# Attention value products widened from 64 to 128 rows, transposes grouped by unit, first score tile at 128 columns

## The chip, the cores and the metric

The kernel runs on one core of a Trainium2 chip. The metric is the device time of one execution in microseconds (us). Three runs of the kernel before took 1123.78, 1124.84 and 1125.99 us; the median, 1124.84 us, is the time that a changed kernel is compared with.

## The reference, cut to what matters

Attention over 4 batches of 8 heads with 576 positions and head size 64, then two feed-forward layers on the 2304 tokens:

```python
scores = q @ k.T / sqrt(64)                       # per batch and head
cum    = cumsum(max(s, 0))                        # per batch and head
bias   = min(-(cum[:, None] - cum[None, :]), 0)
attn   = softmax(where(causal, -1e9, scores + bias))
x      = (attn @ v) as [2304, 512]                # heads side by side
x      = (silu(x @ w_gate) * (x @ w_val)) @ w_out # d_ff 1536
out    = silu(x @ w_in) @ w_out2                  # d_ff 2048
```

All data are float32. The kernel gets the precision of float32 out of the matrix engine by splitting an operand into a high part and the remainder (names ending in `h` and `l`, type fp32r) and adding the products.

## The kernel before, in words

**Attention.** A head's 576 positions are cut into five tiles, `TILES`: the first has 64 positions, the other four 128. A head is worked on in two units: half A is query tiles 0, 1, 2 (320 queries), half B is query tiles 3 and 4 (256 queries). There are 64 units. Each goes through three steps, in three successive slots:

1. `a_scores` (L208 on), once for each query tile: products of the queries and keys (L223), the bias and the running minimum on DVE (L231), the exponential on ACT (L241), the normalisation of `e` on POOL (L116 by way of `copy`). For query tile 0 the stationary operand has 64 columns, one for each query, and 64 key columns stream past it.
2. `a_transpose` (L257 on): PE transposes the 64 or 128 row blocks of `e` (L271) into a PSUM bank, and the bank is emptied into SBUF, ACT writing the high part `ph` (L280) and DVE the remainder `pl` (L281). `GROUPS` says which key tiles share a bank: half A has two groups, half B three. Each group is a piece of work of its own. In batch 0 (`WHOLE_P`) the weights stay float32 in one part, and L114 or L112 empties the bank.
3. `a_pv` (L288 on): for each key tile j the product of its values and the transposed weights, high part and then remainder, all added up in one bank (L299). Key tile 0 has 64 positions, so its two products run over 64 rows, with `vsa` as stationary operand (`vra` in batch 0); the others run over 128 rows with `vsb`. Then ACT and DVE take the sum out (L313, L314).

`a_split` (L178 on) makes the split operands of the next head, `vsa` and `vsb` among them. `ps_a` is the pool of four PSUM banks that scores, transposes and value products share; `pt` has four buffers each for `ph` and `pl`; `e` has six buffers.

**Order.** `slot_pieces(u)` lists the pieces of slot u: the scores of unit u, the split and load of coming heads, the value products of unit u-2, the transposes of unit u-1. The first 18 slots (batch 0 and the start of batch 1) run with no other matrix work. After that the first feed-forward layer runs in 36 chunks of weights, nine for each batch (`gate`, L413 to L415 with `pgv`; `down`, the same lines with `po`), and the pieces of two slots are dealt out between the four or eight steps of a chunk. So the attention of batches 1, 2 and 3 runs between the products of batches 0, 1 and 2. The last nine chunks and the second layer (`up2`, `down2`) have no attention in them.

The program is built with a planner that simulates the engines and may move an instruction that is ready ahead of one that waits for data or a buffer; on each engine the instructions then run in the planned order.

Of the kernel before, what the change touches and what calls it, by code (L numbers as in the profile page):

```python
# [8 lines left out]
F32 = mybir.dt.float32  # L9
F32R = mybir.dt.float32r  # L10
U32 = mybir.dt.uint32
AF = mybir.ActivationFunctionType
ALU = mybir.AluOpType

B, H, S, D = 4, 8, 576, 64
NT, DM = B * S, H * D
F1, F2 = 1536, 2048
P = 128
# [12 lines left out]
TILES = [(0, 64), (64, 128), (192, 128), (320, 128), (448, 128)]  # L31
HALF = {"A": ([0, 1, 2], 0, 320), "B": ([3, 4], 320, 256)}

GROUPS = {"A": [(0,), (1, 2)], "B": [(0,), (1, 2), (3, 4)]}
# [6 lines left out]
WHOLE_P = [(0, h) for h in range(8)]  # L41
# [4 lines left out]
VHI = "agaa"  # L46
# [21 lines left out]
def kernel(  # L68
# [15 lines left out]
    def pool(name, bufs, space=None, scope=ctx, side="left"):  # L84
        kw = {"space": space} if space is not None else {}
        return scope.enter_context(tc.tile_pool(name=name, bufs=bufs, side=side, reuse_waits="tile", **kw))
# [12 lines left out]
    qks_p = pool("qks", 2, scope=attention, side="right")  # L99
    cum_p = pool("cum", 2, scope=attention, side="right")  # L100
    e_p = pool("e", 6, scope=attention, side="right")
    pt_p = pool("pt", 4, scope=attention, side="right")
    v_p = pool("v", 2, scope=attention, side="right")
    xr_p = pool("xr", 2, scope=attention, side="right")
    xq_p = pool("xq", 2, scope=attention, side="right")
# [12 lines left out]

    ident = const.tile([P, P], F32, name="ident")
    make_identity(nc, ident)  # L120
    cum = const.tile([B * H, S], F32, name="cum")
    cum_d = dram.tile([B * H, S], F32, name="cum_d")
    w32 = dram.tile([NGV + NO1, P, CW], F32, name="w32")
    x2_d = dram.tile([KD, P, NT], F32, name="x2_d")
# [19 lines left out]


    st, loads = {}, []

    def a_load(b, h, halves):
        k1, v1, q0 = SPAN[halves]
# [28 lines left out]
    def a_split(b, h, halves):  # L178
        k1, v1, q0 = SPAN[halves]
        t, c, xa, xb = st.pop((b, h, halves))  # L180
        if (b, h) in WHOLE_S:
            ks, qs = t[:D, 1], (t[:D, 0],)
        else:
            ks = qks_p.tile([P, S], F32R, tag="ks", name="ks")
            qh = qks_p.tile([P, S], F32R, tag="qh", name="qh")
            ql = qks_p.tile([P, S], F32R, tag="ql", name="ql")
            qs = (qh, ql)
            copy(KHI[b], ks[:, :k1], t[:, 1, :k1])
            copy(QHI[b], qh[:, q0:k1], t[:, 0, q0:k1])
            eng = nc.gpsimd if b in POOL_KS else nc.vector  # L190
            eng.tensor_tensor(out=ks[D:P, :k1], in0=t[D:P, 1, :k1], in1=ks[D:P, :k1].bitcast(F32), op=ALU.subtract)
            eng = nc.gpsimd if b in POOL_QL else nc.vector
            eng.tensor_tensor(out=ql[:, q0:k1], in0=t[:, 0, q0:k1], in1=qh[:, q0:k1].bitcast(F32), op=ALU.subtract)
        if (b, h) not in WHOLE_P:
            va_s = v_p.tile([64, 2, D], F32R, tag="vsa", name="vsa")
            vb_s = v_p.tile([P, 4, 2, D], F32R, tag="vsb", name="vsb")
            copy(VHI[b], va_s[:, 0, :], xa)
            copy(VHI[b], vb_s[:, :v1, 0, :], xb[:, :v1])
            nc.vector.tensor_tensor(out=va_s[:, 1, :], in0=xa, in1=va_s[:, 0, :].bitcast(F32), op=ALU.subtract)
            eng = nc.gpsimd if b in POOL_V else nc.vector  # L200
            eng.tensor_tensor(
                out=vb_s[:, :v1, 1, :], in0=xb[:, :v1], in1=vb_s[:, :v1, 0, :].bitcast(F32), op=ALU.subtract
            )
            xa, xb = va_s.rearrange("p t d -> p (t d)"), vb_s.rearrange("p j t d -> p j (t d)")
        for half in halves:
            st[b, h, half, "in"] = (ks, qs, c, xa, xb)

    def a_scores(b, h, half, i):  # L208
        ks, qs, c, _, _ = st[b, h, half, "in"]
        q0, r = TILES[i]  # L210
        wd = q0 + r
        e = e_p.tile([P, S], F32, tag="e", name="e")

        g0 = 0 if wd <= 320 else 320
        nc.gpsimd.affine_select(
            out=e[:r, g0:wd], in_=c[:r, g0:wd], pattern=[[-1, wd - g0]], compare_op=ALU.is_ge,
            fill=-8.0 * QMASK, base=q0 - g0, channel_multiplier=1,
        )
        m = None
        for c0, n in ((0, wd),) if wd <= 512 else ((0, g0), (g0, wd - g0)):  # L220
            ps = ps_a.tile([P, 512], F32, tag="a", name="psc")
            for part, q in enumerate(qs):
                nc.tensor.matmul(  # L223
                    out=ps[:r, :n], lhsT=q[:, q0 : q0 + r], rhs=ks[:, c0 : c0 + n],
                    start=(part == 0), stop=(part == len(qs) - 1),
                )
            for g, end, gate in ((c0, min(g0, c0 + n), c), (max(g0, c0), c0 + n, e)):
                if g >= end:
                    continue
                m2 = sm_p.tile([P, 1], F32, tag="m", name="m")  # L230
                nc.vector.tensor_tensor_reduce(  # L231
                    out=e[:r, g:end], in0=ps[:r, g - c0 : end - c0], in1=gate[:r, g:end], scale=-0.125,
                    scalar=3.0e38 if m is None else m[:r], op0=ALU.add, op1=ALU.min, accum_out=m2[:r],
                )
                m = m2

        if i in (0, 1, 3):
            st[b, h, "l"] = sm_p.tile([P, 2], F32, tag="l", name="l")
        l = st[b, h, "l"]
        col = 1 if i in (2, 4) else 0  # L240
        nc.scalar.activation(  # L241
            out=e[:r, :wd], in_=e[:r, :wd], func=AF.Exp, bias=m[:r], scale=-1.0, accum_out=l[:r, col : col + 1]
        )
        st[b, h, "e", i] = e
        if i in (1, 3):
            return
        done = (0,) if i == 0 else (i - 1, i)
        w = len(done)
        rl = sm_p.tile([P, 2], F32, tag="rl", name="rl")
        nc.vector.tensor_scalar(out=l[:r, :w], in0=l[:r, :w], scalar1=1.0e-9, scalar2=None, op0=ALU.add)  # L250
        nc.vector.reciprocal(out=rl[:r, :w], in_=l[:r, :w])  # L251
        for n, j in enumerate(done):
            q0, r = TILES[j]
            e = st[b, h, "e", j]
            copy("g", e[:r, : q0 + r], e[:r, : q0 + r], rl[:r, n : n + 1])

    def a_transpose(b, h, half, js):  # L257
        tiles, base, n = HALF[half]
        ps = ps_a.tile([P, 512], F32, tag="a", name="ptr")
        kw = TILES[js[0]][1]  # L260
        at, put = 0, []
        for j in js:
            k0 = TILES[j][0]
            lo = max(k0, base)
            for i in tiles:
                q0, r = TILES[i]
                if q0 < k0:
                    continue
                e = st[b, h, "e", i]
                o = at + q0 - lo  # L270
                nc.tensor.transpose(ps[:kw, o : o + r], e[:r, k0 : k0 + kw], ident[:r, :r])  # L271
            put.append((j, at, lo - base, base + n - lo))
            at += base + n - lo
        ph = pt_p.tile([P, 512], F32 if (b, h) in WHOLE_P else F32R, tag="ph", name="ph")
        parts = (ph,)
        if (b, h) in WHOLE_P:
            copy("v" if (half, js[0]) in DVE_PT else "a", ph[:kw, :at], ps[:kw, :at])
        else:
            pl = pt_p.tile([P, 512], F32R, tag="pl", name="pl")
            nc.scalar.activation(out=ph[:kw, :at], in_=ps[:kw, :at], func=AF.Copy)  # L280
            nc.vector.tensor_tensor(  # L281
                out=pl[:kw, :at], in0=ps[:kw, :at], in1=ph[:kw, :at].bitcast(F32), op=ALU.subtract
            )
            parts = (ph, pl)
        for j, o, off, width in put:
            st[b, h, "p", half, j] = ([p[:kw, o : o + width] for p in parts], off, width)

    def a_pv(b, h, half):  # L288
        tiles, base, n = HALF[half]
# [226 lines left out]
    def slot_pieces(u):  # L516
        pcs = []
        if u < len(units):
            b, h, half, sp = units[u]
            for i in HALF[half][0]:  # L520
                pcs.append(lambda b=b, h=h, half=half, i=i: a_scores(b, h, half, i))
            if half == sp[0]:
                n = spans.index((b, h, sp))
                if n + 1 < len(spans):
                    pcs.append(lambda x=spans[n + 1]: a_split(*x))
                if n + 2 < len(spans):
                    pcs.append(lambda x=spans[n + 2]: a_load(*x))
        if u >= 2 and u - 2 < len(units):
            x = units[u - 2][:3]
            pcs.append(lambda x=x: a_pv(*x))  # L530
        if 1 <= u and u - 1 < len(units):
            b, h, half, _ = units[u - 1]
            for js in GROUPS[half]:
                pcs.append(lambda b=b, h=h, half=half, js=js: a_transpose(b, h, half, js))
        return pcs

    def w_ahead(c):
# [5 lines left out]

    def body():
        setup()
        a_load(*spans[0])
        a_load(*spans[1])
        a_split(*spans[0])
# [98 lines left out]
```

## Time and profile before

| | |
|---|---|
| runs, us | 1123.78, 1124.84, 1125.99 |
| profiled execution, us | 1128.98, its span 1127.2 |
| mean granted TensorE clock | 0.991 of full |
| PE busy | 1091.4 us (97% of the span), 6760 products |
| PE weight loads (PEld) | 996.5 us |
| DVE, ACT, POOL busy | 726.0, 589.3, 562.7 us |
| packets of DMA queue q1, share of the time of 16 DMA engines | 35.9% |

The profiled execution is one execution; its time is 1.78 us more than its span, and 4.14 us above the median of the runs. A product's duration in the trace overlaps the next one's, since the matrix engine is pipelined; what a product costs there is read from the distance of its start to the next start. In a name such as `64*128 64x320`, the first pair is the stationary operand's rows and columns, the second the streamed operand's.

### The profile page before, as it was taken

How to read it: one execution, taken by the hardware profiler on the slowest of the kernel's cores; microseconds unless marked ns; L12 is line 12 of the kernel's file. 1: busy time of each engine (PE TensorE's matmuls, PEld its weight loads, DVE VectorE, ACT ScalarE, POOL GpSimd, SP SyncE). 2: the span in 40 equal slices, each digit the busy share in tenths (PEclk: the TensorE clock that was granted, in tenths of full speed). 3: DMA queues.
4: the chain of work that ended last, by engine and by line, in shares of the span. 5: the costliest groups of instructions: out<-in, count | busy, mean ns of one | idle time of the engine just before them, and what ended most of it. 6: DMA issues, size and time to landing. Idle time of an engine off the chain costs nothing. (4 is left out here: it accounts for less than half of the span.)

```text
span 1127.2 us, 19389 instructions
## 1 busy us (share of the span) xinstructions
PE 1091.4 (97%) x6760; PEld 996.5 (88%) x6760; DVE 726.0 (64%) x1625; ACT 589.3 (52%) x1294; POOL 562.7 (50%) x603
## 2 busy tenths in 40 slices
PE   6988998999999999999999999999999999999998
PEld 4556887989999999999999999989888898988887
DVE  6777999897787887777755435734463646544333
ACT  4877887765666654666644434565242323422221
POOL 5668889895575755665632533333323232232221
PEclk9988999999999999999999999999999999999999
DMA  5587666665344445352216231721120101000012
GB/s 133 139 240 237 191 219 199 209 197 154 112 110 115 112 112 155 83 141 65 76 54 203 85 102 63 242 69 43 34 74 19 57 19 56 19 1 1 1 57 112
DMA packets 53728, 121.39 MB, mean 108 GB/s; under 512 B 8256, under 2 KB 21568, under 8 KB 53632
## 3 DMA queue, kind: packets, MB, share of 16 engines
q1 hardware_dynamic: 53632, 120.17, 35.9%
q8 instruction: 53, 0.87, 0.3%
q14 instruction: 43, 0.35, 0.1%
HBM read 101.20 MB, written 18.95 MB: 107 GB/s over the span
## 5 line engine op out<-in xcount | busy, mean ns | idle before, releaser
L428 POOL TENSOR_TENSOR h<-u,h 128x288 fp32r<-128x288 f32 (+2 forms) x176 | 192.7, 1096 | 341.0 <-ACT h L112 338.7
L413 PE MATMUL pgv<-xt,wh 128*128 128x288 f32 x768 | 231.7, 302 | 3.0 <-DVE u L424 3.0
L413 PE MATMUL po<-h,wh 128*128 128x288 f32 (+2 forms) x704 | 232.7, 332 | 1.2 <-ACT h L112 1.2
L414 PE MATMUL po<-h,wh 128*128 128x288 f32 (+2 forms) x704 | 233.1, 331 | 0.0
L415 PE MATMUL po<-h,wl 128*128 128x288 f32 (+2 forms) x704 | 231.9, 330 | 0.0
L414 PE MATMUL pgv<-xt,wh 128*128 128x288 f32 x768 | 229.2, 299 | 1.3 <-DVE xt L320 1.3
L415 PE MATMUL pgv<-xt,wl 128*128 128x288 f32 x768 | 229.0, 298 | 0.0
L402 POOL TENSOR_TENSOR wl<-wraw,wh 128x1024 fp32r<-128x1024 f32 x53 | 129.9, 2453 | 83.4 <-ACT wh L112 82.7
L413 PEld LDWEIGHTS pgv<-xt,wh 128*128 128x128 f32 x768 | 146.0, 190 | 4.5 <-DVE u L424 3.9
L414 PEld LDWEIGHTS pgv<-xt,wh 128*128 128x128 f32 x768 | 146.1, 190 | 1.8 <-DVE xt L320 1.5
L415 PEld LDWEIGHTS pgv<-xt,wl 128*128 128x128 f32 x768 | 145.8, 190 | 0.3 <-issue 0.2
L424 DVE SCALAR_TENSOR_TENSOR u<-th,pu 128x464 f32<-128x464 f32 (+1 forms) x80 | 50.6, 633 | 138.7 <-ACT th L422 138.7
L413 PEld LDWEIGHTS po<-h,wh 128*128 128x128 f32 x704 | 132.0, 188 | 8.8 <-ACT h L112 2.0
L415 PEld LDWEIGHTS po<-h,wl 128*128 128x128 f32 x704 | 132.2, 188 | 6.9
L414 PEld LDWEIGHTS po<-h,wh 128*128 128x128 f32 x704 | 132.3, 188 | 6.7 <-POOL h L428 0.4
L112 ACT ACTIVATE h<-u 128x288 fp32r<-128x288 f32 (+2 forms) x176 | 89.1, 506 | 88.9 <-DVE u L424 50.4
L116 POOL TENSOR_SCALAR e<-e,rl 64x64 f32<-64x64 f32 (+4 forms) x160 | 101.9, 647 | 57.6 <-DVE rl L251 42.5
L508 DVE SCALAR_TENSOR_TENSOR acc<-po,acc 128x464 f32<-128x464 f32 (+1 forms) x140 | 88.4, 636 | 61.8 <-PE po L415 61.3
L422 ACT ACTIVATE th<-pu 128x464 f32<-128x464 f32 (+1 forms) x80 | 44.1, 551 | 151.2 <-PE pu L415 151.2
L112 ACT ACTIVATE wh<-wraw 128x1024 fp32r<-128x1024 f32 x88 | 92.1, 1055 | 54.5 <-PE po L414 35.4
L414 PE MATMUL pu<-x,wh 128*128 128x464 f32 (+1 forms) x320 | 118.9, 371 | 0.0
L241 ACT ACTIVATE e<-e,m 64x64 f32<-64x64 f32 (+4 forms) x160 | 89.1, 557 | 56.9 <-DVE m L231 55.9
(83 smaller groups left out, 2122.2 us busy)
## 6 DMA issues: line engine op xcount, KB each, us to landing
wraw<-w SPq DMA_DIRECT2D x54, 512.0 KB, 4.5
r<-in_w_dram SPq DMA_DIRECT2D x52, 512.0 KB, 4.9
qkr<-in_qk_dram SPq DMA_DIRECT2D x64, 288.0 KB, 4.6
w<-wraw SPq DMA_DIRECT2D x18, 512.0 KB, 3.9
cumb<-cum_d SPq DMA_DIRECT2D x30, 288.0 KB, 3.4
r<-in_w_dram SPq DMA_DIRECT2D x32, 256.0 KB, 3.1
x_d<-acc SPq DMA_DIRECT2D x32, 144.0 KB, 3.9
vrb<-in_vb_dram SPq DMA_DIRECT2D x32, 128.0 KB, 4.0
```

The source lines that it names most:

```text
L112: nc.scalar.activation(out=out, in_=in_, func=AF.Copy, scale=scale)
L116: nc.gpsimd.tensor_scalar(out=out, in0=in_, scalar1=scale, scalar2=1.0, op0=ALU.mult, op1=ALU.mult)
L241: nc.scalar.activation(out=e[:r, :wd], in_=e[:r, :wd], func=AF.Exp, bias=m[:r], scale=-1.0, accum_out=l[:r, col : col + 1])
L402: engines[eng].tensor_tensor(out=wl, in0=t, in1=wh.bitcast(F32), op=ALU.subtract)
L413: nc.tensor.matmul(out=ps[:, :n], lhsT=a, rhs=xh, start=(k == 0), stop=False)
L414: nc.tensor.matmul(out=ps[:, :n], lhsT=a, rhs=xl, start=False, stop=False)
L415: nc.tensor.matmul(out=ps[:, :n], lhsT=c, rhs=xh, start=False, stop=(k == last))
L422: nc.scalar.activation(out=th[:, :n], in_=pg[:, :n], func=AF.Tanh, scale=0.5)
L424: nc.vector.scalar_tensor_tensor(out=u, in0=th[:, :n], scalar=1.0, in1=pg[:, :n], op0=ALU.add, op1=ALU.mult)
L428: engines[LO[ph]].tensor_tensor(out=lo, in0=u, in1=hi.bitcast(F32), op=ALU.subtract)
L508: nc.vector.scalar_tensor_tensor(out=a, in0=ps[:, :n], scalar=0.5, in1=a, op0=ALU.mult, op1=ALU.add)
```

## The change

Four things are done.

- The value operand and the transposed weights of key tile 0 get 128 rows, of which rows 64 to 127 are zero, in batches 1 to 3. The buffers for this (three of `vsa`, one pair `ph`, `pl` for half A and one for half B) are filled with zeros once, on POOL, by `zeros()` right after `setup()`, and only their first 64 rows are written afterwards.
- `a_transpose` takes a whole unit: all transposes of its two or three groups are issued first, each group in its own bank, and then the banks are emptied.
- The score products always use 128 query columns, so query tile 0 computes 128 columns of which 64 are used.
- Buffers: `pt` has three buffers instead of four, and `cum` lies in the pool `e`.

```diff
-    pt_p = pool("pt", 4, scope=attention, side="right")
+    pt_p = pool("pt", 3, scope=attention, side="right")
+    zero_p = pool("zero", 1, scope=attention, side="right")
-    cum = const.tile([B * H, S], F32, name="cum")
+    cum = e_p.tile([B * H, S], F32, tag="e", name="cum")
+    first_v, first_p = [], []
+
+    def zeros():
+        z = e_p.tile([P, S], F32, tag="e", name="z")
+        nc.gpsimd.memset(z[D:P], 0.0)
+        for n in range(3):
+            va_s = zero_p.tile([P, 2, D], F32R, tag=f"v0_{n}", name="vsa")
+            copy("g", va_s[D:P], z[D:P, : 2 * D].rearrange("p (t d) -> p t d", t=2))
+            first_v.append(va_s)
+            if n == 2:
+                break
+            both = []
+            for part in "hl":
+                t = zero_p.tile([P, 320], F32R, tag=f"p{part}0_{n}", name=f"p{part}0")
+                copy("g", t[D:P], z[D:P, :320])
+                both.append(t)
+            first_p.append(both)
 # a_split
-            va_s = v_p.tile([64, 2, D], F32R, tag="vsa", name="vsa")
+            va_s = first_v[(b * H + h) % 3]
-            copy(VHI[b], va_s[:, 0, :], xa)
+            copy(VHI[b], va_s[:D, 0, :], xa)
 # a_scores
-                    out=ps[:r, :n], lhsT=q[:, q0 : q0 + r], rhs=ks[:, c0 : c0 + n],
+                    out=ps[:, :n], lhsT=q[:, q0 : q0 + P], rhs=ks[:, c0 : c0 + n],
 # a_transpose: the transposes of a group as before, then
-    def a_transpose(b, h, half, js):
+    def a_transpose(b, h, half):
+        done = []
+        for js in GROUPS[half]:
...
+            done.append((js, ps, kw, at, put))
+        for js, ps, kw, at, put in done:
+            whole = (b, h) in WHOLE_P
+            if js == (0,) and not whole:
+                ph, pl = first_p["AB".index(half)]
+                rows = P
+            else:
+                ph = pt_p.tile([P, 512], F32 if whole else F32R, tag="ph", name="ph")
+                pl = None if whole else pt_p.tile([P, 512], F32R, tag="pl", name="pl")
+                rows = kw
...
+                st[b, h, "p", half, j] = ([p[:rows, o : o + width] for p in parts], off, width)
 # slot_pieces
-            for js in GROUPS[half]:
-                pcs.append(lambda b=b, h=h, half=half, js=js: a_transpose(b, h, half, js))
+            pcs.append(lambda b=b, h=h, half=half: a_transpose(b, h, half))
 # body
         setup()
+        zeros()
```

## Rows read from the trace of the kernel before

**Rows 1.** Busy time of each engine in three stretches (us from the start).

```profile
0.00:80.00 80.00, 65.05 (x302) 41.75 (x303) 59.07 (x193) 55.68 (x148) 48.90 (x91) 0.95 0.62 161
80.00:255.00 175.00, 161.74 (x1106) 146.05 (x1105) 155.12 (x382) 131.99 (x304) 152.93 (x154) 0.97 0.69 212
255.00:610.00 355.00, 353.26 (x2620) 339.14 (x2618) 266.37 (x677) 208.99 (x505) 201.47 (x240) 1.00 0.40 114
```

**Rows 2.** Timeline of PE: a value product of half B, batch 3 (start, duration).

```profile
406.73 0.29 PE L414 MATMUL po<-h,wh 128*128 128x288 f32 x1
406.87 0.29 PE L415 MATMUL po<-h,wl 128*128 128x288 f32 x1
407.09 0.38 PE L299 MATMUL pv<-ph,vsa 64*128 64x256 f32 x1
407.31 0.28 PE L299 MATMUL pv<-pl,vsa 64*128 64x256 f32 x1
407.51 0.39 PE L299 MATMUL pv<-ph,vsb 128*128 128x256 f32 x1
407.74 0.28 PE L299 MATMUL pv<-pl,vsb 128*128 128x256 f32 x1
407.86 0.28 PE L299 MATMUL pv<-ph,vsb 128*128 128x256 f32 x1
```

**Rows 3.** Timeline of the weight loads, same place.

```profile
407.09 0.18 PEld L299 LDWEIGHTS pv<-ph,vsa 64*128 64x128 f32 x1 [0.17 <-PE po L414]
```

**Rows 4.** Timeline of PE: a value product of half A.

```profile
416.49 0.41 PE L299 MATMUL pv<-ph,vsa 64*128 64x320 f32 x1
416.74 0.31 PE L299 MATMUL pv<-pl,vsa 64*128 64x320 f32 x1
416.97 0.39 PE L299 MATMUL pv<-ph,vsb 128*128 128x256 f32 x1
417.20 0.28 PE L299 MATMUL pv<-pl,vsb 128*128 128x256 f32 x1
```

**Rows 5.** Instructions on the tile vsa between 255 and 640 us.

```profile
L299 PE MATMUL pv<-ph,vsa x33: 381/384/412, 263.7 to 587.6; 64*128 64x256 f32 x17, 64*128 64x320 f32 x16
```

**Rows 6.** PE and weight loads, timeline: the first score tile of a head.

```profile
412.50 0.19 PE L223 MATMUL psc<-ks,qh 128*64 128x64 f32 x1
412.55 0.19 PEld L413 LDWEIGHTS pgv<-xt,wh 128*128 128x128 f32 x1
412.80 0.30 PE L414 MATMUL pgv<-xt,wh 128*128 128x288 f32 x1
```

**Rows 7.** Timeline of PE: a run of six transposes, and two runs of three.

```profile
408.59 0.91 PE L271 MATMUL ptr<-ident,e 64*64 64x64 f32 x6
409.47 0.29 PE L414 MATMUL pgv<-xt,wh 128*128 128x288 f32 x1
428.03 0.58 PE L271 MATMUL ptr<-ident,e 64*64 64x64 f32 x3
428.59 0.30 PE L413 MATMUL po<-h,wh 128*128 128x288 f32 x1
429.12 0.49 PE L271 MATMUL ptr<-ident,e 128*128 128x128 f32 x3
429.58 0.29 PE L415 MATMUL po<-h,wl 128*128 128x288 f32 x1
```

**Rows 8.** Timelines of ACT and DVE: emptying a bank of transposes.

```profile
421.50 0.60 ACT L280 ACTIVATE ph<-ptr 128x512 fp32r<-128x512 f32 x1 [1.54 <-PE ptr L271]
422.14 0.69 DVE L281 TENSOR_TENSOR pl<-ptr,ph 128x512 fp32r<-128x512 f32 x1 [0.61 <-ACT ph L280]
```

**Rows 9.** Waits between 80 and 260 us: total, times, longest.

```profile
PE ptr L271 <- POOL e L116: 5.9, 7, 1.4
```

**Rows 10.** POOL: its idle stretch at the start, and a copy's mean (ns).

```profile
6.94 1.40 POOL L193 TENSOR_TENSOR ql<-qkr,qh 128x576 fp32r<-128x576 f32 x1 [5.63 <-DVE qh L114]
L116 POOL TENSOR_SCALAR e<-e,rl 128x320 f32<-128x320 f32 x32 | 17.2, 538 | 0.0
```

More of the change, by code (lines that the diff above doesn't have):

```diff
@@ L194, in a_split @@
         if (b, h) not in WHOLE_P:
-            va_s = v_p.tile([64, 2, D], F32R, tag="vsa", name="vsa")
+            va_s = first_v[(b * H + h) % 3]
             vb_s = v_p.tile([P, 4, 2, D], F32R, tag="vsb", name="vsb")
-            copy(VHI[b], va_s[:, 0, :], xa)
+            copy(VHI[b], va_s[:D, 0, :], xa)
             copy(VHI[b], vb_s[:, :v1, 0, :], xb[:, :v1])
-            nc.vector.tensor_tensor(out=va_s[:, 1, :], in0=xa, in1=va_s[:, 0, :].bitcast(F32), op=ALU.subtract)
+            nc.vector.tensor_tensor(out=va_s[:D, 1, :], in0=xa, in1=va_s[:D, 0, :].bitcast(F32), op=ALU.subtract)
             eng = nc.gpsimd if b in POOL_V else nc.vector
@@ L255, in a_scores @@
             copy("g", e[:r, : q0 + r], e[:r, : q0 + r], rl[:r, n : n + 1])
-    def a_transpose(b, h, half, js):
+    def a_transpose(b, h, half):
         tiles, base, n = HALF[half]
[L259 to L286, printed above, removed]
@@ new lines, in a_transpose @@
+        done = []
+        for js in GROUPS[half]:
+            ps = ps_a.tile([P, 512], F32, tag="a", name="ptr")
+            kw = TILES[js[0]][1]
+            at, put = 0, []
+            for j in js:
+                k0 = TILES[j][0]
+                lo = max(k0, base)
+                for i in tiles:
+                    q0, r = TILES[i]
+                    if q0 < k0:
+                        continue
+                    e = st[b, h, "e", i]
+                    o = at + q0 - lo
+                    nc.tensor.transpose(ps[:kw, o : o + r], e[:r, k0 : k0 + kw], ident[:r, :r])
+                put.append((j, at, lo - base, base + n - lo))
+                at += base + n - lo
+            done.append((js, ps, kw, at, put))
@@ new lines, in a_transpose @@
+        for js, ps, kw, at, put in done:
[7 more added lines that the diff above has]
+                rows = kw
+            parts = (ph,)
+            if whole:
+                copy("v" if (half, js[0]) in DVE_PT else "a", ph[:kw, :at], ps[:kw, :at])
+            else:
+                nc.scalar.activation(out=ph[:kw, :at], in_=ps[:kw, :at], func=AF.Copy)
+                nc.vector.tensor_tensor(
+                    out=pl[:kw, :at], in0=ps[:kw, :at], in1=ph[:kw, :at].bitcast(F32), op=ALU.subtract
+                )
+                parts = (ph, pl)
+            for j, o, off, width in put:
+                st[b, h, "p", half, j] = ([p[:rows, o : o + width] for p in parts], off, width)
```

## The prediction

> **What bounds the kernel now.** I read the busy times by stage first. Between 255 and 610 us PE is busy 353.26 of 355 us at full clock, DVE 266.37, ACT 208.99, POOL 201.47 [rows 1]: there PE alone sets the pace, and what shortens PE's work shortens the kernel. Between 80 and 255 us PE is still first with 161.74 of 175, but DVE (155.12) and POOL (152.93) are close behind it [rows 1]: an engine that is handed less work there may just wait longer. In the first 80 us PE is busy 65.05 of 80 [rows 1]. This is batch 0, whose value products the change leaves at 64 rows. After 610 us there is no attention, so nothing of the change acts there.
>
> Second came the timeline of PE inside the middle stage. A busy PE is not PE at its peak, so I read distances between starts. Two gate products of 288 columns start 0.14 us apart (406.73, 406.87), and two value products of 256 columns over 128 rows 0.12 apart (407.74, 407.86) [rows 2]. Around the two products of key tile 0, the distances are longer: 406.87 to 407.09, 0.22; to 407.31, 0.22; to 407.51, 0.20; to 407.74, 0.23 [rows 2]. The weight loads tell why. The load for the first `vsa` product begins only at 407.09, after its queue sat idle for 0.17 us until the product before had ended [rows 3]. Elsewhere a load runs under the product before it. So going from 128 rows to 64 empties the pipeline and then leaves a load uncovered, and going back to 128 rows does it again. Half A shows the same: 0.25, 0.23 and 0.23 us [rows 4].
>
> **The change part by part.**
>
> *Value products of key tile 0.* With 128 rows the columns streamed stay the same, so the products should start at the distances of their neighbours. Half B: 0.22 becomes 0.14, 0.22 becomes 0.12, 0.20 becomes 0.12, 0.23 becomes 0.12; together 0.87 becomes 0.50, a gain of 0.37 us for a unit [rows 2]. Half A: 256 columns take 0.12, so 320 take about 0.15, an estimate; 0.25 and 0.23 become 0.15 each, 0.23 becomes 0.12, and the entry gains 0.08 as in half B; together 0.37 [rows 2, 4]. Batches 1 to 3 have 24 heads, so 48 units; 33 of them start after 255 us [rows 5]. There the gain is whole: 33 x 0.37 = 12.2 us. The 15 earlier units could give 15 x 0.37 = 5.6 us, or nothing if DVE and POOL decide; PE is the busiest of the three, so I take two thirds, 3.7 us.
>
> *First score tile with 128 query columns.* The streamed work stays at 64 columns; the weight load doubles. Now the pair and the gate product behind it take 412.50 to 412.80, 0.30 us; less 0.14 for the gate product that leaves 0.16 for the pair [rows 6, 2]. The nearest row for a load of 128 columns in front of a short product is the run of three transposes of 128 columns: 429.12 to 429.58, less 0.14, is 0.32, or 0.11 each [rows 7, 2]. A pair would then take 0.22, that is 0.06 more for a head; 32 heads, 1.9 us. From below it costs nothing; I take 1.5, since PE is not the bound everywhere.
>
> This is where a rule speaks for a larger gain. In the trace the load of the gate weights behind the 64-column pair starts at 412.55, 0.05 us after the first of the pair, with no idle time in front of it [rows 6]: a stationary operand of 64 columns does not empty the pipeline, one of 64 rows does. The Trainium skill (TensorEngine Tiling (Array Packing), Tiling Modes, Key Properties) says that changing the tiling mode drains the engine, and counts 128x64 among the modes as it does 64x128. By that rule this edit would take away two drains for each head, and the sum would be lower, as the rival on columns below says; by the row it costs.
>
> *Transposes in one run.* A run of six takes 408.59 to 409.47, 0.88, less 0.14: 0.74. Two runs of three take 428.03 to 428.59 (0.42) and 429.12 to 429.58 (0.32), also 0.74 [rows 7, 2]. So a longer run saves nothing of PE's own time: I take 0. The 64-row transpose of query tile 0 stays, with its drain. What moves is the place: with fewer pieces in a chunk, the transposes of half B come later behind the scores, and those of its first group no longer stand a step ahead of the rest. Between 80 and 260 us PE stood 5.9 us, 7 times, before a transpose that waited for POOL's normalisation [rows 9]; this could shrink, a gain of at most 5.9. Against it, a run in half B holds three of the four banks of `ps_a` at once, and a bank is free only after ACT and DVE have emptied it, 0.60 and 0.69 us for the widest [rows 8]. Behind a PE instruction that waits for a bank everything on PE is queued. In the middle stage the planner has gate products, which use other banks, to put in front of it. Net 0.
>
> *Zeros and buffers.* One memset and seven copies on POOL; the nearest row is 0.54 us for 128x320, so 8 x 0.54 = 4.3 us. POOL sits idle for 5.63 us before its first work of the attention [rows 10], and this covers them. If they ran in front of the first score tile's masks instead, up to 4.3 us. The zeros' first readers are in batch 1. `pt` loses a buffer, but key tile 0 no longer uses it in batches 1 to 3: a head needs three and has three. In batch 0 a head fills five in turn out of three; the one refilled was read by the value products that stand directly ahead of these transposes on PE. If that order fails, ACT's copy waits and the value products behind it on PE; I take 0.
>
> *Sum.* -12.2 - 3.7 + 1.5 = -14.4 us. Against the profiled execution's 1128.98 (span 1127.2 and 1.78 around it) that gives 1114.6. The median of the runs stands 4.14 lower, so on its scale 1124.84 - 14.4 = 1110.4; I say 1110.5. A difference under 0.2% (2.2 us) can't be told from none here.
>
> **The rivals.**
>
> *The early part swallows its share.* The 15 early units give nothing, since DVE and POOL are at 89% and 87% there, and the new order costs a few us in batch 0, where a run holding three banks has no gate product to cover it, or the zeros spill: -12.2 + 1.9 + up to 4.3 = -6 to -10, so 1115 to 1119. Against it: PE is the busiest there too.
>
> *The waits on POOL go as well.* -12.2 - 5.6 - 5.9 + 0 to 1.5 = -22 to -24; a part of that gives 1101 to 1105. For it: the later place of half B's transposes. Against: POOL's work is no less.
>
> *Banks decide (the other side).* In each half B the next score tile or value product stands behind the run of nine transposes and waits for the first bank: 0.60 + 0.69 = 1.29 us [rows 8], once for each of 32 heads, 41 us if nothing covers it. Over 14.4 / 32 = 0.45 us for a head the kernel is slower. At half to the whole price: +6 to +27, so 1131 to 1152. For it: the emptying of the first bank now stands behind the whole run in program order, and both copying engines also serve the gates. Against it: each engine gets the same work in the same sequence as before, and two of the three banks were already filled in one run (408.59, a run of six) [rows 7].
>
> *It doesn't do what it says.* The gap at `vsa` comes from a wait for its data and not from the rows. Then nothing is gained: 1124 to 1127. Against it: the second gap, between `vsa` and `vsb`, follows inside one unit on data long there.
>
> *Columns drain too.* By the rule above two drains and uncovered loads for each first score tile go as well, priced like the rows' 0.37: 32 x 0.37 = 11.8 instead of a cost of 1.5, so 1124.84 - 15.9 - 11.8 = 1097. Rows 6 speak against it.
>
> **How the numbers follow.** Forecast (1105 to 1115) 0.56; early part swallows 0.15; waits go as well 0.12; banks 0.09; nothing gained 0.05; columns drain 0.03. The predicted time is the first's, 1110.5. From 1102 to 1119 hold the first, the second and most of the third, some 0.80; the bounds of the terms (-5.6 to 0 early, 0 to 1.9 for the columns, -5.9 to 0 for the waits, 0 to 4.3 for the zeros) span about the same. Faster: 0.56 + 0.15 + 0.12 + 0.03 = 0.86; the case of nothing gained is the same, 0.05; banks are slower, 0.09.
>
> **What would show it.** Right: `vsa` products appear as 128*128, the next start 0.12 to 0.15 us behind each, no idle weight load ahead of them; the stage of the second and third attention batches shorter by about 12 us at the same number of products; the first score pair about 0.06 us longer; transposes at 0.11 each whatever the run. Wrong: PE idle behind DVE `pl` or ACT `ph` ahead of a score tile (banks); the same 0.2 us distances at 128 rows (not the rows); a start of the first score product later than before (zeros); the gain of the middle stage given back before 255 us, or at the end of the attention near 610 us.

## The result, and the profile after

The changed kernel took 1114.67 us (median of four runs, 1112.31 to 1115.62), the kernel before on the same chip 1124.9: ratio 0.9906, interval 0.9888 to 0.9924, so 10.2 us faster, within 8.5 and 12.6. Forecast were 14.4 us less and 1110.5. A second set of five runs, beside another set of the kernel before, gave 1112.08 against 1124.76, ratio 0.9883 (0.9866 to 0.9901). The two intervals overlap. The profiled execution of the changed kernel took 1114.81 us, its span 1113.0.

Timeline of PE in the changed kernel, a value product of half B (start, duration, line, operands); it answers to [rows 2]:

```profile
418.68 0.30 PE L442 MATMUL po<-h,wh 128*128 128x288 f32 x1
418.81 0.28 PE L328 MATMUL pv<-ph,vsa 128*128 128x256 f32 x1
418.93 0.28 PE L328 MATMUL pv<-pl,vsa 128*128 128x256 f32 x1
419.05 0.28 PE L328 MATMUL pv<-ph,vsb 128*128 128x256 f32 x1
419.17 0.28 PE L328 MATMUL pv<-pl,vsb 128*128 128x256 f32 x1
```

The four distances between starts are 0.13, 0.12, 0.12 and 0.12, together 0.49 us where they were 0.87 [rows 2]. The weight loads there no longer wait for an empty pipeline; this one, at the start of such a value product, runs under the gate product that begins at 418.68, where before the queue sat idle for 0.17 us [rows 3]:

```profile
418.69 0.19 PEld L328 LDWEIGHTS pv<-ph,vsa 128*128 128x128 f32 x1
```

The first score tile, as timeline of PE; it answers to [rows 6]:

```profile
404.83 0.19 PE L242 MATMUL psc<-ks,qh 128*128 128x64 f32 x1
404.86 0.27 PE L242 MATMUL psc<-ks,ql 128*128 128x64 f32 x1
404.97 0.38 PE L442 MATMUL pgv<-xt,wh 128*128 128x288 f32 x1
405.18 0.30 PE L443 MATMUL pgv<-xt,wh 128*128 128x288 f32 x1
```

The pair and the gate product behind it take 404.83 to 405.18, 0.35 us, where they took 0.30: 0.05 more for a head, with 0.06 forecast.

A run of nine transposes, all that half B has, and the gate products behind it:

```profile
413.15 1.15 PE L292 MATMUL ptr<-ident,e 128*64 128x128 f32 x9
414.06 0.38 PE L442 MATMUL pgv<-xt,wh 128*128 128x288 f32 x1
414.28 0.30 PE L443 MATMUL pgv<-xt,wh 128*128 128x288 f32 x1
```

From 413.15 to 414.28, less 0.13 for the gate product, it is 1.00 us, 0.11 each, as in the runs of three and six [rows 7].

Busy times by stage, answering to [rows 1] (the last stretch ends at 600 here):

```profile
0.00:80.00 80.00, 66.60 (x307) 43.59 (x308) 60.43 (x194) 55.94 (x148) 55.74 (x99) 0.96 0.62 164
80.00:255.00 175.00, 158.91 (x1123) 147.49 (x1123) 159.65 (x389) 133.00 (x309) 153.36 (x157) 0.98 0.70 215
255.00:600.00 345.00, 344.20 (x2632) 339.48 (x2630) 258.71 (x676) 208.04 (x502) 201.17 (x240) 1.00 0.41 119
```

PE still fills the middle stage. Between 80 and 255 us DVE (159.65) is now as busy as PE (158.91). Two waits of PE between 80 and 275 us (total, times, longest) moved against each other:

```profile
PE ptr L292 <- POOL e L117: 3.7, 6, 0.9
PE psc L242 <- DVE x L343: 4.0, 4, 2.1
```

The transposes' wait for POOL was 5.9 [rows 9]; the wait of a score tile for a bank that DVE is still emptying of value products (L343 here, L314 before) was 1.8 us in the kernel before.

Fixed times cut the stages differently in each kernel. For all that follows I therefore counted the products of the feed-forward layer in the timeline of PE (L413 to L415 before, called gate products here; 864 for a batch) and took two landmarks: the start of the first one of batch 1 and of the first one of batch 3. Between them, in every run, lie 1728 gate products, the value products of 32 units, and the first score tile and first transposes of 15 heads, all in the PE-bound stage. This is called the middle. The third column is what is left of the span.

```
profiled execution      to batch 1   middle         rest
before                  277.98       323.76         525.5
before, second profile  277.23       323.76         523.3
changed                 274.77       313.46         524.8
changed, second         275.18       313.38         520.9
```

The middle column repeats to 0.1 us. It holds 10.3 us of the gain. The other two vary by some us from execution to execution.

### The profile page after: what moved, and what is told of

The parts are those of the page before. It is cut to its first block, busy times and chain, and to the rows that moved or that the text cites. A ratio compares the mean times of both kernels' runs of the same rounds, so it can differ in the third digit from the quotient of the medians.

```text
span 1113.0 us, 19360 instructions
## 1 busy us (share of the span) xinstructions
PE 1076.9 (97%) x6760; PEld 995.5 (89%) x6760; DVE 721.6 (65%) x1625; ACT 588.2 (53%) x1294; POOL 568.5 (51%) x611
## 5 line engine op out<-in xcount | busy, mean ns | idle before, releaser
L457 POOL TENSOR_TENSOR h<-u,h 128x288 fp32r<-128x288 f32 (+2 forms) x176 | 200.2, 1139 | 353.7 <-ACT h L113 343.9
L443 PE MATMUL pu<-x,wh 128*128 128x464 f32 (+1 forms) x320 | 118.8, 371 | 0.0
L442 PE MATMUL pu<-x,wh 128*128 128x464 f32 (+1 forms) x320 | 118.5, 370 | 0.0
```

The source lines that it names most:

```text
L442: nc.tensor.matmul(out=ps[:, :n], lhsT=a, rhs=xh, start=(k == 0), stop=False)
L443: nc.tensor.matmul(out=ps[:, :n], lhsT=a, rhs=xl, start=False, stop=False)
L457: engines[LO[ph]].tensor_tensor(out=lo, in0=u, in1=hi.bitcast(F32), op=ALU.subtract)
```

## The experiments

All ran with the kernel before on the same chip; medians of the runs and the ratio's interval are given, and the landmarks of each profile.

**The kernel before, again.** No edit.

> The kernel before, unchanged, for a second profile. If its first profiled execution (1128.98 us) was just a slow one, this one lies near the median of 1124.9 us, and the stretch in which it is some 4 us shorter shows which part varies from execution to execution; I expect the first 275 us, where the clock was below full, or the stop of 2.3 us near 610 us. If the profiler itself slows this kernel, it is near 1129 again.

Its median was 1126.38 us against 1125.39 in the shared runs of the same kernel (ratio 1.001, 0.9998 to 1.0021), its profiled execution 1126.09. So the profiler doesn't slow it, and the first profiled execution (1128.98) was one of the longer ones: 0.75 us went in the stage up to batch 1, none in the middle, 2.2 in the rest. So a single execution varies by some 3 us outside the middle.

**Wide value products alone.** The zero buffers and 128 rows; transposes by group and 64 columns as before. The creation of the buffers is left out here.

```diff
-            va_s = v_p.tile([64, 2, D], F32R, tag="vsa", name="vsa")
+            va_s = first_v[(b * H + h) % 3]
...
+        first = js == (0,) and (b, h) not in WHOLE_P
+        if first:
+            ph, pl = first_p["AB".index(half)]
+            rows = P
```

> Only the value products of key tile 0 over 128 rows, with the zero buffers; transposes by group and the first score tile at 64 columns as before. Theory (a change of rows empties PE's pipeline): 10 to 15 us under before, so 1110 to 1115, at least as fast as the whole change; the products of key tile 0 start 0.12 to 0.15 us before the next. Rival (the gain of the whole change came from the order of the transposes): under 3 us, 1122 or more. Rival (the gap was a wait for data): the gaps of 0.2 us stay, 1123 to 1126.

1112.96 us, ratio 0.9885 (0.9871 to 0.9899): 12.4 us faster. Landmarks 275.43, 311.11, 525.5. In the middle that is 12.65 us less for 32 units, 0.395 each, with 0.37 forecast.

**Grouped transposes alone.** The grouping inside `a_transpose` is that of the whole change and is left out here.

```diff
-            for js in GROUPS[half]:
-                pcs.append(lambda b=b, h=h, half=half, js=js: a_transpose(b, h, half, js))
+            pcs.append(lambda b=b, h=h, half=half: a_transpose(b, h, half))
...
```

> Only the transposes of a unit in one run; 64 rows, 64 columns and four pt buffers as before. Theory: a run of n transposes costs n x 0.11 us however it is cut, so within 3 us of before, 1122 to 1128. Rival (order): 5 us or more faster, since the stop near 610 us and the waits on POOL go. Rival (banks): slower by 5 us or more.

1125.06 against 1125.39 us, ratio 0.9995 (0.9984 to 1.0006): no difference. Landmarks 277.71, 324.58, 522.7: the middle is 0.8 us longer. The timeline of PE shows where this comes from. In the kernel before (second profile), half A's transposes stand directly behind the value products of half B:

```profile
333.21 0.28 PE L299 MATMUL pv<-pl,vsb 128*128 128x128 f32 x1
333.41 0.58 PE L271 MATMUL ptr<-ident,e 64*64 64x64 f32 x3
333.75 0.38 PE L415 MATMUL po<-h,wl 128*128 128x288 f32 x1
```

With grouped transposes, the planner puts gate products between the two:

```profile
333.81 0.27 PE L305 MATMUL pv<-pl,vsb 128*128 128x128 f32 x1
333.92 0.35 PE L420 MATMUL po<-h,wh 128*128 128x288 f32 x1
334.10 0.29 PE L421 MATMUL po<-h,wl 128*128 128x288 f32 x1
...
335.16 0.29 PE L420 MATMUL po<-h,wh 128*128 128x288 f32 x1
335.38 0.58 PE L273 MATMUL ptr<-ident,e 64*64 64x64 f32 x3
```

A gate product behind a value product of 128 columns starts on time, but the next one follows after 0.18 instead of 0.13 us (333.92 to 334.10); that its load is not covered by the short product is my reading. The emptying in front of the 64-row transposes is there in both, 0.09 us beyond the usual distance (0.20 against 0.11; 0.22 against 0.13). Counted over the middle, a gate product stands directly behind such a value product 17 times, where it was 4 times in the kernel before: 13 exits more at 0.05 us make 0.7 of the 0.8.

**128 query columns alone.**

```diff
-                    out=ps[:r, :n], lhsT=q[:, q0 : q0 + r], rhs=ks[:, c0 : c0 + n],
+                    out=ps[:, :n], lhsT=q[:, q0 : q0 + P], rhs=ks[:, c0 : c0 + n],
```

> Only the score products with 128 query columns. Theory (a load of 128 columns is 0.05 to 0.06 us longer, 32 heads): 0 to 2 us slower than before, 1125 to 1127. Rival (a change of columns drains as well): about 12 us faster, 1113.

1129.85 us, ratio 1.0034 (1.0021 to 1.0047): 4 us slower, twice what I had expected at most. Landmarks 280.49, 324.81, 523.7. The middle is 1.05 us longer, 0.07 for each of its 15 first score tiles, where 0.06 was priced. The other 3 us were lost before batch 1. There the products come in another order than in the kernel before, and waits of PE between 80 and 255 us changed (total, times, longest): in the kernel before (second profile)

```profile
PE psc L223 <- DVE x L314: 1.8, 2, 0.9
PE psc L223 <- DVE m L231: 1.0, 2, 0.6
```

and with 128 columns

```profile
PE psc L223 <- DVE x L314: 4.9, 4, 2.0
PE psc L223 <- DVE m L231: 2.5, 4, 1.1
```

L314 is the instruction with which DVE empties a bank of value products; a score tile behind it waits for that. That columns drain is refuted: the kernel is 4 us slower where that rule gave 12 faster, and the middle is 1.05 longer where it gave 15 x 0.37 = 5.6 less.

**The changed kernel reading 64 rows.** All buffers, order and columns of the changed kernel; only the operands are cut.

```diff
-            vv = wa if j == 0 else wb[:, j - 1]
+            vv = wa[:D] if j == 0 else wb[:, j - 1]
...
-                st[b, h, "p", half, j] = ([p[:rows, o : o + width] for p in parts], off, width)
+                st[b, h, "p", half, j] = ([p[:kw, o : o + width] for p in parts], off, width)
```

> The changed kernel with everything as it is (zero buffers, transposes in one run, 128 query columns), but the products of key tile 0 read only the first 64 rows of the same buffers. Theory (the rows): all the gain of the rows goes, about 13 us, and 128 columns alone cost 4 us in the run before, so 1126 to 1130; the 0.2 us distances are back. Rival (a wait for the data of the old buffers made the gaps): it stays near the changed kernel's 1114.7.

1124.54 us, ratio 0.9995 (0.9984 to 1.0006): the whole gain is gone, though the time is 1.5 us under the band I gave, since I had added the 4 us of the run before, 3 of which belonged to its early stage. Landmarks 274.78, 325.25, 522.1. In the middle that is 11.8 us more than the changed kernel, 0.37 for each of the 32 units. The old distances are back, 0.23, 0.25, 0.24 and 0.22 us:

```profile
417.26 0.29 PE L444 MATMUL pgv<-xt,wl 128*128 128x288 f32 x1
417.49 0.41 PE L328 MATMUL pv<-ph,vsa 64*128 64x320 f32 x1
417.74 0.31 PE L328 MATMUL pv<-pl,vsa 64*128 64x320 f32 x1
417.98 0.39 PE L328 MATMUL pv<-ph,vsb 128*128 128x256 f32 x1
418.20 0.28 PE L328 MATMUL pv<-pl,vsb 128*128 128x256 f32 x1
```

The data and the buffers are those of the changed kernel, and PE's instructions come in the same order from the first to the last; the number of rows is the only thing that differs. A wait for the data as cause is refuted, and so is the order.

This run also shows what the rows were worth before batch 1, with 16 units there: next to nothing. Its landmark at batch 1 is 274.78, the changed kernel's 274.77 and 275.18. From the first gate product to that landmark it takes 196.6 us (from 78.2), the changed kernel 195.2 and 195.7, so 0.9 to 1.4 us of 16 x 0.37 = 5.9 remain. PE stood idle for 12.7 us between 80 us and the landmark with 64 rows, and for 16.1 and 15.9 with 128.

**The changed kernel with 64 columns.** The edit of the columns undone.

```diff
-                    out=ps[:, :n], lhsT=q[:, q0 : q0 + P], rhs=ks[:, c0 : c0 + n],
+                    out=ps[:r, :n], lhsT=q[:, q0 : q0 + r], rhs=ks[:, c0 : c0 + n],
```

> The changed kernel with 64 query columns for the first score tile. Theory (the columns only cost): 1 to 4 us under the changed kernel, so 1111 to 1114, like the run with wide value products alone. Rival (columns and rows are worth something together): equal to the changed kernel or slower, 1115 or more.

1114.15 us, ratio 0.9897 (0.9883 to 0.9911), not to be told from the changed kernel in total, and between the two bands expected. Landmarks 277.33, 312.87, 522.9: the middle is 0.6 us shorter, the early stage 2.2 to 2.6 longer than the changed kernel's.

**128 rows through to the transposes.** On top of the wide value products, the first query tile keeps its 128 rows, so the 64-row transposes go as well.

```diff
         wd = q0 + r
+        r = P
...
-                nc.tensor.transpose(ps[:kw, o : o + r], e[:r, k0 : k0 + kw], ident[:r, :r])
+                nc.tensor.transpose(ps[:kw, o : o + P], e[:, k0 : k0 + kw], ident)
```

> Wide value products, transposes by group, and the first query tile carried through with 128 rows (scores, masks, exponential, normalisation), so that its 64-row transpose becomes a 128-row one whose surplus 64 columns the next transpose overwrites. Theory (any change of rows empties the pipeline): the two emptyings around the transposes of half A go, 0.2 us for a head, less 0.06 for the 128 columns: 17 heads in the PE-bound stage give 2.4 us, all 32 give 4.5; 1108 to 1111 against 1113.0 for the wide value products alone. Rival (only matmuls of fp32r drain, not transposes; the columns cost): 1114 to 1117.

1115.16 us, ratio 0.9916 (0.99 to 0.9933): in total inside the rival's band. Landmarks 280.95, 309.28, 522.6: the mechanism is right where PE sets the pace, 1.8 us less than with wide value products alone, and the early stage lost 5.5 us. Half A's transposes, behind the value products:

```profile
423.84 0.28 PE L326 MATMUL pv<-pl,vsb 128*128 128x128 f32 x1
423.95 0.50 PE L291 MATMUL ptr<-ident,e 128*64 128x128 f32 x3
424.20 0.38 PE L442 MATMUL po<-h,wl 128*128 128x288 f32 x1
```

The entry takes 0.11 and the three 0.25 us, where they took 0.20 and 0.34 at 333.21 in the kernel before: 0.18 for a head. The stationary operand has 64 columns in both, so transposes empty the pipeline at a change of rows too.

**The same, and batch 0's value products over 128 rows.** The buffers for the values and the weights are left out here.

```diff
         if first:
             ph, pl = first_p["AB".index(half)]
             rows = P
+            if (b, h) in WHOLE_P:
+                ph = whole_w["AB".index(half)]
...
```

> As e128, and batch 0's value products of key tile 0 over 128 rows as well (float32, zero rows in buffers of their own). Theory: 16 units more lose two changes of rows each, 0.4 us; PE is busy 65 of the first 80 us, so half to all of 6 us is left, 1102 to 1108. Rival (batch 0 is set by ACT, DVE and POOL): within 1 us of e128.

1112.52 us, from 1108.67 to 1119.78, ratio 0.9892 (0.9862 to 0.9922): inconclusive. The interval, 1109.8 to 1116.6 us, lies above the theory's band and holds the rival's, but the median is 2.6 us under the run without it, outside the 1 us that the rival allows. The landmark at batch 1 (279.72) is 1.2 us earlier than without it, which speaks for the rival; the profiled execution lost 6 us in the rest (529.0).

**Remainder products of batch 1 left out.** On top of the wide value products. The attention of batch 1 is then computed with less precision.

```diff
+            if b == 1:
+                qs = qs[:1]
             for part, q in enumerate(qs):
...
+            if b == 1:
+                ps = ps[:1]
             for part, pp in enumerate(ps):
```

> The wide value products alone (as in the run with only them), and in batch 1 the remainder products of scores and value products are left out (its attention has less precision; DVE, ACT and POOL do the same work). By the distances between starts this takes 0.77 + 0.87 = 1.6 us from PE for each of 8 heads, 13 us, all of it before 275 us. Theory A (PE sets the pace there too, as I assumed with two thirds): 8 to 13 us under the wide value products' 1113, so 1100 to 1105. Theory B (in that stretch DVE, POOL and the planned order decide, and PE's gains are swallowed): 0 to 4 us under, 1109 to 1114.

1111.48 us, ratio 0.9879 (0.9857 to 0.9901), 1.5 us under the run with wide value products alone: theory B. Landmarks 275.20, 311.10, 525.8. Batch 1's first product comes no earlier than with the 13 us still on PE (275.43). Busy times in steps of 5 us (columns: stretch, length, PE, PEld, DVE, ACT, POOL, granted clock, DMA share, GB/s):

```profile
240.00:245.00 5.00, 3.52 (x29) 3.22 (x28) 5.00 (x13) 4.36 (x12) 5.00 (x3) 1.00 0.94 283
245.00:250.00 5.00, 5.00 (x40) 4.99 (x39) 5.00 (x14) 2.69 (x7) 5.00 (x8) 1.00 0.46 130
250.00:255.00 5.00, 5.00 (x41) 4.77 (x40) 4.83 (x4) 4.95 (x12) 5.00 (x4) 1.00 0.92 315
255.00:260.00 5.00, 1.55 (x8) 1.32 (x7) 4.86 (x13) 1.35 (x5) 3.96 (x7) 0.75 0.20 66
260.00:265.00 5.00, 5.00 (x25) 5.00 (x24) 4.34 (x15) 1.53 (x5) 3.57 (x4) 0.57 0.85 225
```

and the wait of PE in the middle of it:

```profile
PE psc L244 <- DVE m L252: 3.4, 1, 3.4
```

DVE is busy 19.69 of the 20 us from 240 to 260, where it was 17.37 with the wide products alone. PE, which had run ahead, stands still for 3.4 us. In the 5 us from 260 its granted clock is 0.57, most of it at the lower of its two levels (1.2 GHz). What PE had won is gone by batch 1: between 80 and 275 us its waits for DVE ahead of score tiles add up to 12.8 us, against 4.6 with the wide products alone.

**128 rows to the transposes in batches 2 and 3 only.**

```diff
+        if b >= 2:
+            r = P
...
```

> As the run with 128 rows of the first query tile carried through to the transposes, but only in batches 2 and 3, so that the plan of the first 255 us stays near that of the wide value products alone. Theory (the loss of that run lay in the reordered first 255 us; in the PE-bound stage each head gains 0.2 us at the transposes and pays 0.06 for the columns): about 2 us under the wide value products' 1113, so 1109.5 to 1112. Rival (128 rows there don't help): 1113 or more.

1110.74 us, from 1110.47 to 1111.24, ratio 0.9874 (0.9856 to 0.9892), as the theory had it. Landmarks 274.85, 309.28, 524.9: the early stage is that of the wide products, the middle 14.5 us shorter than before and 4.1 shorter than the changed kernel's. In total it has the lowest median of all, 1.3 us under the changed kernel on the same chip, but their intervals overlap.

**The changed kernel, again.** No edit.

> The changed kernel again, beside these two and the kernel before on one chip: 1112 to 1116, a ratio of about 0.990; its second profile shows whether the stop of 1.9 us and the half clock behind it, at the start of the second layer, come in every execution (then about 1114.7 in each) or only in some (then this profile is some 2 us shorter there).

1112.08 us, ratio 0.9883 (0.9866 to 0.9901). In the first profile, the chain that ended last runs at the start of the second layer through a transfer:

```profile
711.91 5.65 DMA x2r<-x_d
...
719.24 0.72 PE po L442
719.96 0.39 PE po L444
720.35 0.39 PE po L442
```

PE waited 1.9 us, and the granted clock was 0.52 in the next 3.2 us, close to its lower level, with products 0.39 us apart instead of 0.21:

```profile
719.20:722.40 3.20, 3.16 (x8) 2.76 (x9) 2.12 (x5) 3.20 (x7) 1.18 (x1) 0.52 0.37 131
```

In the second, the same transfer took 4.63 us, PE waited 0.9 us and the clock stayed at full (2.4 GHz):

```profile
711.27 4.63 DMA x2r<-x_d
...
PE po L442 <- ACT h L113: 0.9, 1, 0.9
...
719.00:722.00 3.00, 3.00 (x16) 2.67 (x15) 2.59 (x5) 3.00 (x7) 0.37 (x1) 1.00 0.05 16
```

So a stop of this length, and the half clock, come in some executions only; of the 3.9 us by which the rest of the two profiles differs, the piece around it makes 2.7 (counted between the same two products).

The length of a stop does not decide about the clock by itself. Near 229 us PE waits 2.1 us for the same bank in both profiles. In the first the clock stays at full behind it, in the second it falls:

```profile
229.40:232.00 2.60, 2.31 (x17) 2.08 (x17) 2.56 (x10) 1.50 (x5) 2.51 (x5) 1.00 0.38 88
...
229.80:232.40 2.60, 2.31 (x11) 2.08 (x11) 2.56 (x10) 1.50 (x5) 2.51 (x5) 0.62 0.37 89
```

## Why the prediction was right, and where it was off

*What bounds the kernel, and the cause of the gaps:* right. The same buffers and order with 64 rows cost all of the gain, and 0.37 to 0.395 us for a unit came out of the middle where 0.37 stood in the sum. One reading was loose: the row of the idle weight load names the product before the last (L414), not the last, as what it waited for [rows 3].

*33 units for 12.2 us:* the wide products alone took 12.65 us from 32 units.

*The transposes at "net 0":* this step failed by a small size. A transpose costs 0.11 us in any run, as said, but I had counted runs and not their neighbours. The value products and the transposes were one run of short products before; now gate products often come between. That is 0.8 us in the middle by itself. On top of the wide products it measured 1.76 (312.87 against 311.11). Of that the 13 exits more make 0.7 again, and one wait of a score tile for a bank with value products makes 0.5 (at 408.9 us; it is there in both profiles of the changed kernel as well, and in neither of the runs with one of the two edits alone). The other 0.6 I did not find.

*128 columns at 0.06:* 0.07 by itself; 0.6 us in the middle on top of the other edits, 0.04 for each of 15 heads. The sum of the three for the middle, as forecast, was 32 x 0.37 - 15 x 0.06 = 10.9 us; it measured 10.3.

*15 early units at two thirds, 3.7 us:* this term failed. PE was the busiest engine there, but that does not make it the one that sets the pace. With the order unchanged the rows gave 0.9 to 1.4 us at most before batch 1, and nothing by the landmark itself; 13 us less work for PE moved the landmark by 0.2 (275.43 to 275.20). What PE won turned for the greater part into waits for DVE and POOL. The landmark did move by 2.0 to 2.5 us against the second profile of before, about what 3.7 less the columns would give. That agreement is luck: the run with 64 rows has the same 2.5 us, 1.6 of it before the first gate product (78.2 against 79.8). From edit to edit the landmark lies between 2.5 us earlier (changed kernel) and 3.7 later (128 rows to the transposes); that the order makes this is my reading and not shown by itself. My rival of the early part had the right engines, and its size (nothing gained) was near.

*What the sum left out:* it took everything behind 610 us as fixed. There the profiled executions differ by up to 8 us (520.9 to 529.0), by the stops of PE at the end of the attention and at the start of the second layer. The first profile of the changed kernel had one of these with half the clock behind it. Whether the total comes out at 10.2 us, as in the first set, or at 12.7, as in the second, is for a part decided there.

*Zeros:* in the run with wide products PE's first product waits for POOL until 6.0 us instead of 5.4 for DVE; nothing of it can be seen at the first gate product (80.1 us there, 79.6 and 79.5 in the changed kernel, 80.7 and 79.8 before). *Waits on POOL and banks:* both side effects came, small and against each other. Between 80 and 275 us the transposes' waits for POOL fell from 5.9 to 3.7 us, and the waits of score tiles for a bank with value products rose from 1.8 to 4.0 (2.8 and 4.4 in the second profile). Grouping alone changed nothing that can be measured in total.

## What to carry to other kernels

In a stage in which the matrix engine has no idle time, keep the number of rows the same from one product to the next and pad the odd one with zeros: each change of rows cost about 0.09 us of emptying and 0.1 us for a weight load that nothing covers. What a long run of 64-row products would cost inside, no run here shows. Price such an edit from distances between starts, and count the neighbours of what is moved: a gate product behind value products of 128 columns cost 0.05 us more. Where a planner orders the program, trust the price only in the stage with one bound. In the stage with two near bounds the same rows gave a quarter of their price or less, and edits that differ little came out 2.5 us earlier to 3.7 later.

## What the runs showed of the hardware that was not expected

- A change of rows drains in transposes as in products: 0.18 us for the pair of changes around a 64-row transpose. A change of the stationary operand's columns does not; 128 columns instead of 64 lengthen the load (0.13 to 0.19 us in the trace) and cost 0.04 to 0.07 us for a pair of products.
- A stop of 1.9 us of PE was followed by some 3 us at half the clock, one of 0.9 us at the same place by none; but of two stops of 2.1 us at the same place in two executions, one was followed by a granted clock of 0.62 for 2.6 us and one by full clock.
- The middle repeats to 0.1 us between executions (323.76 and 323.76; 313.46 and 313.38), and kernels with the same order there agree on different chips (311.11 and 311.10; 309.28 and 309.28), while the runs of one kernel lie 0.8 to 11 us apart.
